# First LayerNorm's shift and scale: three of five chunks from TensorE's row matmuls to multiply-and-add on VectorE and GpSimd

## The chip, the cores and the metric

The kernel runs on one core of a Trainium2 chip. The metric is the time of one execution on the device in microseconds, as the median of several runs; smaller is better. A profiled execution gives the trace from which the rows below are taken; it has its own time, which differs a little from the median. TensorE does the matmuls (in the profile PE, and PEld for the loads of the stationary operand), VectorE is DVE, ScalarE is ACT, GpSimd is POOL; SP issues most DMAs.

## The reference

A transformer block with adaptive LayerNorm on 2048 tokens of width 640: linear attention with a Hedgehog feature map (32 heads of 20), then a dense layer with squared ReLU. What the change touches is how `h`'s shift `sa` and scale `ca` come about:

```python
x = A_x                                         # (1, 2048, 640)
mod = (_silu(c) @ w_mod).reshape(c.shape[0], 6, 1, -1)   # c: (1, 640), w_mod: (640, 3840)
sa, ca, ga, sb, cb, gb = (mod[:, 0], mod[:, 1], mod[:, 2], mod[:, 3], mod[:, 4], mod[:, 5])
h = _layernorm(x, axis=-1) * (1 + ca) + sa
x = x + ga * _A_ref(h, A_wqkv, A_w_phi, A_wo)   # q, k, v = h @ wqkv; q and k go through w_phi
h = _layernorm(x, axis=-1) * (1 + cb) + sb
x = x + gb * _B_ref(h, B_w1, B_b1, B_w2, B_b2)
```

## The kernel before

The 2048 tokens are 16 tiles of 128, worked through in pairs (8 blocks of 256); the 640 channels are 5 chunks of 128. Products are made in three passes of rounded fp32 (high by high, high by low, low by high), so each operand exists as a high part, written by ScalarE, and a low part, the difference, made by VectorE (helper `lo`, line 90).

The prologue, up to the first q matmuls, is written out by hand: under `tc.manual_schedule` each engine runs its instructions in the order of the code, and an instruction that waits holds up everything behind it on its engine. It goes so:

- `WARM` matmuls of a tile of ones (line 625) while the first weights travel.
- `fold(nm, d)`: the weights of k, then of q, chunk by chunk, are multiplied with the feature map (line 282), ScalarE takes the high part out of PSUM (line 289), VectorE the low part. The first fold waits for the block-diagonal tile `bd_t`, which VectorE builds (lines 250 and 255).
- `stats` of the first token block (lines 560 to 565: VectorE's bn_stats, then four tiny operations on GpSimd that give `sqa` and `nba`), then `scale` on ScalarE (line 570) normalises it in place.
- The shift and scale of chunk d, as two columns of `cols_a`: `w_ss` holds for each chunk a 128 x 1280 tile `WM[d]`, in which columns 256 k + 128 s + n are the weights from input chunk k to output channel n, s = 0 for the shift, 1 for the scale. `mod_rows2(d)` multiplies it with silu(c) (`cs`, one column for each k) in ten matmuls of 32 output rows each (line 586, tile `mrow`). `mod_sb(d)` copies the rows to SBUF on ScalarE (line 594, tile `msb`) and adds the 1 of (1 + ca); `mod_cols2(d)` transposes them on TensorE (line 599) and sums them on VectorE (line 601) into `cols_a`.
- `out0(d)`: ScalarE applies shift and scale to the transposed chunk (line 375, `hfa`), rounds it to the high part of `hT` (line 376), VectorE makes the low part.
- `k_step(d)`: twelve matmuls that add chunk d to the k of both token tiles (line 80, `pk`). All four PSUM buffers of the tag `pj` are in use by them; the first q matmuls (`pq`) take the first of them over, so they wait for ScalarE's eviction of k (line 433). Ahead of these evictions ScalarE has the scaling of the second token block (`scale(XB[1])`) and the high part of the first v weights (line 667).

The statistics of the second token block (`stats(XB[1], "a1")`) are written behind `k_step(1)`. The loads stand in one order on SP's queue: k weights, the first token block, q weights, `WM[0]` and `WM[1]`, the last q weights, `WM[2]` to `WM[4]`, the second token block, v weights, `b_t`. Eight semaphores are used in turn, so a load is issued only when the one eight places ahead has landed.

Of the kernel before, what the change touches and what calls it, by code (L numbers as in the profile page):

```python
# [8 lines left out]
F32 = mybir.dt.float32  # L9
# [3 lines left out]
ALU = mybir.AluOpType  # L13
AX = mybir.AxisListType

P = 128
# [6 lines left out]
NC = D // P  # L23
# [8 lines left out]
VCOLS = [*range(360), *range(600, 624), *range(360, 600), *range(624, D)]  # L32
EPS = 1e-5
POSTPONED = 4
WARM = 9
KEPT = NT - POSTPONED
W2_AT = 48
PLAIN = 2
# [15 lines left out]
def kernel(  # L54
# [19 lines left out]
    nc = tc.nc  # L74
# [14 lines left out]
    def lo(out_lo, full, hi, eng=None):  # L89
        (eng or nc.vector).tensor_tensor(out_lo, full, hi.bitcast(F32), op=ALU.subtract)  # L90
# [7 lines left out]
    const = ctx.enter_context(tc.tile_pool(name="const", bufs=1))  # L98
# [20 lines left out]
    def row(tag, name):  # L119
        return (pc if tag in ("s3", "s4") else mem).tile([P, D], F32, tag=tag, name=name, bufs=BUFS[tag])  # L120
# [4 lines left out]
    def wslot(name, tag="w", pool=None):  # L125
        return tok2(tag, name, W2_AT if name.startswith("w2_") else 0, pool).bitcast(F32R)
# [10 lines left out]
    def pj(name):  # L137
        return [psA.tile([P, 512], F32, tag="pj", name=f"{name}_{h}", bufs=4) for h in range(2)]

    def tp(name):  # L140
        return psA.tile([P, 512], F32, tag="tp", name=name)
# [10 lines left out]
    ones = const.tile([P, P], F32, name="ones")  # L152
# [19 lines left out]
    cols_a = const.tile([P, 10], F32, name="cols_a")  # L172
# [38 lines left out]
    raw, WM, RV, XB = {}, {}, {}, {}  # L211
# [10 lines left out]
    def load_x(j):  # L222
        XB[j] = tok2(f"x{j % 2}", f"xb{j}")
        nc.sync.dma_start(XB[j], x[256 * j : 256 * j + 256].rearrange("(i p) d -> p i d", p=P))
# [34 lines left out]

    cs = const.tile([P, NC], F32, name="cs")  # L260
    ce = const.tile([P, NC], F32, name="ce")
    const.tile([P, 8], F32, name="fill")
    nc.scalar.activation(ce, c_t, AF.Exp, scale=-1.0)
    nc.vector.tensor_scalar(ce, ce, 1.0, None, op0=ALU.add)
    nc.vector.reciprocal(ce, ce)
# [6 lines left out]
    def fold(nm, d, p=None):  # L272

        w = wslot(f"w{nm}{d}")
        W[nm, d] = w
        p = p or pj(f"fold{nm}{d}")
        for g, (o, n) in enumerate(GR):
            if g < 5:
                r = raw[nm][d // 2][:120, d % 2, g * P : (g + 1) * P]
            else:  # L280
                r = raw[nm][2][:120, 1, d * P : (d + 1) * P]
            nc.tensor.matmul(  # L282
                p[g // 3][:, (g % 3) * 120 : (g % 3) * 120 + n], r, bd_t[:120, g * 120 : g * 120 + n],
                start=True, stop=True,
            )

        def split():
            for h, (a, b) in enumerate(((0, 360), (360, 640))):
                nc.scalar.activation(w[:, 0, a:b], p[h][:, : b - a], AF.Copy)
                lo(w[:, 1, a:b], p[h][:, : b - a], w[:, 0, a:b])  # L290

        return split
# [68 lines left out]
    def t_in(xn, d, p, mixed=False):  # L361
        for i in range(2):
            src = by_turn(xn[:, i])[:, d] if mixed else xn[:, i, d * P : (d + 1) * P]
            nc.tensor.transpose(p[:, i * P : (i + 1) * P], src, ident)  # L364
# [7 lines left out]
    def t_out(cols, hT, d, nm, p, hf=None):  # L372
        if hf is None:
            hf = row("s3", f"hf{nm}_{d}")[:, :256]
        nc.scalar.activation(hf, p[:, :256], AF.Identity, bias=cols[:, d : d + 1], scale=cols[:, 5 + d : 6 + d])
        nc.scalar.activation(hT[:, d, 0], hf, AF.Copy)
        lo(hT[:, d, 1], hf, hT[:, d, 0])
# [43 lines left out]
    def do_v(t):  # L421
        v_out(t, proj("v", t))
# [40 lines left out]
    def do_q(t, *between):  # L463
        q_out(t, proj("q", t, *between))
# [103 lines left out]
    def scale(xt, nb, sq):  # L568
        for i in range(2):
            nc.scalar.activation(xt[:, i], xt[:, i], AF.Identity, bias=nb[:, i : i + 1], scale=sq[:, i : i + 1])  # L570

    def half(b, h):
        return kvp[b][:, 256 * h : 256 * h + 256]
# [3 lines left out]
    def mod_rows2(*ds):  # L577

        p = tp(f"mrow{ds[0]}")
        for m, d in enumerate(ds):  # L580
            MR[d] = p[:, m * P : m * P + P]
            for k in range(NC):
                for s in range(2):
                    c = 2 * (k % 2) + s
                    a = 256 * k + P * s
                    nc.tensor.matmul(  # L586
                        MR[d][32 * c : 32 * c + 32], cs[:, k : k + 1].to_broadcast([P, 32]), WM[d][:, a : a + P],
                        start=(k < 2 and m == 0), stop=(k >= NC - 2), skip_group_check=True,
                    )

    def mod_sb(*ds):
        for d in ds:
            t = MR[d, "sb"] = row("s1", f"msb{d}")[:, :P]
            nc.scalar.activation(t, MR[d], AF.Identity, bias=plus[:, 0:1])

    def mod_cols2(*ds):
        at = {d: half(0, 1)[:, P * (d % 2) : P * (d % 2) + P] for d in ds}
        for d in ds:
            nc.tensor.transpose(at[d], MR[d, "sb"], ident)
        for d, p in at.items():  # L600
            nc.vector.tensor_reduce(
                cols_a.rearrange("p (s d) -> p s d", s=2)[:, :, d],
                p.rearrange("p (h s r) -> p s h r", h=2, s=2)[:, :, :, 0], axis=AX.X, op=ALU.add,
            )

    TR = [half(0, 0), half(1, 0), half(1, 1), half(2, 0), half(2, 1)]
    mem.tile([P, 48], F32, tag="gap", name="gap", bufs=1)
    HT[0], HT[1] = ht("hT0", 0), ht("hT1", 1)
# [11 lines left out]
    def out0(d):  # L620
        t_out(cols_a, HT[0], d, "a0", TR[d])

    warm = tp("warm")
    for i in range(WARM):
        nc.tensor.matmul(warm[:, :P], ones, ones, start=True, stop=True)  # L625
# [4 lines left out]
    fold("q", 0, kvp[1:])()  # L630
    fold("q", 1)()
    scale(XB[0], *n0)
    fold("q", 2)()
    split = fold("q", 3)
    mod_rows2(0)
    mod_sb(0)
    for d in range(NC):
        t_in(XB[0], d, TR[d])
    split()
    mod_cols2(0)  # L640
    out0(0)
    mod_rows2(1)
    mod_sb(1)
    split = fold("q", 4)
    mod_cols2(1)
    split()
    mod_rows2(2)
    mod_sb(2)
    load_x(2)
    PP += [pj(f"pk{t}") for t in range(2)]  # L650
    rows_at, cols_at = {1: (3, 4)}, {1: (2,), 2: (3, 4)}
    for d in range(NC):
        mod_cols2(*cols_at.get(d, ()))
        if d + 1 < NC:
            out0(d + 1)
        if d in rows_at:
            mod_rows2(*rows_at[d])
        k_step(d)
        mod_sb(*rows_at.get(d, ()))
        if d == 1:  # L660
            n1 = stats(XB[1], "a1")
        if d == 3:
            scale(XB[1], *n1)
# [25 lines left out]
    for d in range(NC):  # L689
        t_in(XB[1], d, TR[d])  # L690
    t_out(cols_a, HT[1], 0, "a1", TR[0])
    t_out(cols_a, HT[1], 1, "a1", TR[1])
    do_q(1)
    exps(EK[1])
    k_norm(EK[0], 0)
    for d in range(2, NC):
        t_out(cols_a, HT[1], d, "a1", TR[d])
    do_v(0)
# [14 lines left out]
    for t in range(2, NT - 2):  # L713
# [13 lines left out]
        p = proj("v", t, *([(1, 0, lambda: t1(j + 1, 4))] if t == NT - 3 else []))  # L727
# [492 lines left out]
    for j in range(NB):  # L1220
# [65 lines left out]
        if j == 7:  # L1286
            t2(0, 4)
            p = tp("gbt")[:NC, :P]
# [512 lines left out]
```

## Time and profile before

| | |
|---|---|
| median of 3 runs | 751.55 us (751.29 to 751.74) |
| the profiled execution | 751.83 us, span 750.1 us |
| TensorE busy | 744.9 us, 99% of the span |
| VectorE, ScalarE, GpSimd busy | 601.4, 457.5, 169.0 us |
| granted TensorE clock | 1.0 over the span |

A row of the timeline reads: start in us from the span's start, length in us, engine, line, operation, output<-inputs, shape, how many were merged, and in brackets how long the engine was idle before and what ended that. A row of a group by line has, after the count, the busy time in us and the mean duration of one in ns, and after the second bar the idle time ahead of them with its cause. In rows of a single line three durations stand as least/median/most. A fp32 matmul shows as two passes, so x20 is ten matmuls.

### The profile page before, as it was taken

The numbers are of one execution on the slowest core, as the hardware profiler recorded it, in microseconds if no ns is written. First come the engines' busy times: TensorE is split into PE (matmuls) and PEld (weight loads), VectorE is DVE, ScalarE is ACT, GpSimd is POOL, SyncE is SP. The second block draws the span as 40 slices with busy tenths as digits, with TensorE's granted clock in tenths as the row PEclk, the third lists the DMA queues.
The fourth block names the chain that finished last, engine by engine and source line by source line (L and its number), as shares of the span: only waits on it lengthen the run. The fifth ranks groups of instructions, "written<-read, shape, count | busy, mean of one in ns | idle before, by whom it ended". The sixth has DMA issues, their size and how long they took to land.

```text
span 750.1 us, 15320 instructions
## 1 busy us (share of the span) xinstructions
PE 744.9 (99%) x5854; PEld 728.3 (97%) x5854; DVE 601.4 (80%) x1089; ACT 457.5 (61%) x1065; POOL 169.0 (23%) x355
## 2 busy tenths in 40 slices
PE   9999999999999999999999999999999999999998
PEld 9999999999999998998999999999999999999997
DVE  6598987988998899999665778777777776777766
ACT  5767666667863355557587766475574756647431
POOL 3000101000100237647303040132221313223110
PEclk9999999999999999999999999999999999999999
DMA  9811432343432254663885576797667767667461
GB/s 330 335 36 77 155 93 81 107 140 107 137 101 81 57 189 160 150 148 109 195 236 183 158 212 227 252 343 204 180 198 200 222 183 227 191 172 218 127 184 36
DMA packets 58796, 126.39 MB, mean 168 GB/s; under 512 B 7438, under 2 KB 16403, under 8 KB 58723
## 3 DMA queue, kind: packets, MB, share of 16 engines
q1 hardware_dynamic: 38636, 79.20, 32.2%
q0 software_dynamic: 17504, 40.90, 21.8%
q10 hardware_dynamic: 2583, 5.30, 1.9%
q8 instruction: 46, 0.75, 0.4%
q14 instruction: 27, 0.22, 0.1%
HBM read 100.74 MB, written 29.89 MB: 174 GB/s over the span
## 4 chain that ended last, share of the span: by engine, by line
PE 98%; ACT 1%; DVE 1%; POOL 0%; issue 0%; ACTq 0%; POOLq 0%
PE up L80 25%; PE acc L80 18%; PE pq L80 9%; PE pk L80 9%; PE pv L80 9%; PE pwo L80 9%; PE acc3x L80 5%; PE kvp L457 3%; PE te L954 2%; PE numa L80 1%; PE foldk L282 1%; PE numb L80 1%; PE ta L364 1%; PE foldq L282 1%; PE warm L625 1%; PE mrow L586 1%
## 5 line engine op out<-in xcount | busy, mean ns | idle before, releaser
L80 PE MATMUL up<-h,w 128*128 128x256 f32 x1640 | 204.6, 276 | 0.1
L80 PEld LDWEIGHTS up<-h,w 128*128 128x128 f32 x1640 | 196.5, 188 | 0.7 <-DVE h L90 0.5
L1350 ACT ACTIVATE ft<-up,b_t 128x256 f32<-128x256 f32 x104 | 49.0, 471 | 96.0 <-PE up L80 95.6
L80 PE MATMUL acc<-w,ra 128*128 128x384 f32 x452 | 97.5, 335 | 0.0
L80 PE MATMUL pwo<-wo,ot 128*128 128x384 f32 (+1 forms) x480 | 78.4, 314 | 0.0
L1351 DVE TENSOR_TENSOR ft<-ft 128x256 f32<-128x256 f32 x104 | 43.8, 421 | 43.1 <-ACT ft L1350 41.4
L80 PE MATMUL pq<-wq,hT 128*128 128x384 f32 (+1 forms) x480 | 75.6, 312 | 0.0
L80 PEld LDWEIGHTS acc<-w,ra 128*128 128x128 f32 x452 | 72.7, 188 | 0.8 <-DVE ra L90 0.6
L80 PE MATMUL pk<-wk,hT 128*128 128x384 f32 (+1 forms) x480 | 72.7, 308 | 0.0
L80 PEld LDWEIGHTS pwo<-wo,ot 128*128 128x128 f32 x480 | 69.7, 188 | 2.8 <-issue 2.7
L80 PEld LDWEIGHTS pq<-wq,hT 128*128 128x128 f32 x480 | 71.1, 188 | 0.6 <-issue 0.2
L80 PE MATMUL pv<-wv,hT 128*128 128x384 f32 (+1 forms) x480 | 71.6, 306 | 0.0
L80 PEld LDWEIGHTS pk<-wk,hT 128*128 128x128 f32 x480 | 70.5, 188 | 0.4 <-issue 0.2
L80 PEld LDWEIGHTS pv<-wv,hT 128*128 128x128 f32 x480 | 70.0, 188 | 0.0
L90 DVE TENSOR_TENSOR ra<-ft,ra 128x384 fp32r<-128x384 f32 (+2 forms) x86 | 36.8, 449 | 32.6 <-ACT ra L1374 20.0
L1460 POOL DMA_DIRECT2D ring_a<-td_a x34 | 18.5, 543 | 116.9 <-PE acc L80 103.6
L1374 ACT ACTIVATE ra<-ft 128x384 fp32r<-128x384 f32 x48 | 25.2, 526 | 28.4 <-DVE ft L1351 22.4
L80 PE MATMUL acc3x<-w,ra 128*128 128x256 f32 x231 | 39.5, 278 | 0.0
L80 PEld LDWEIGHTS acc3x<-w,ra 128*128 128x128 f32 x231 | 37.2, 188 | 0.0
L1365 DVE TENSOR_TENSOR ft<-ft 128x128 f32<-128x128 f32 x136 | 33.3, 286 | 1.2
L448 DVE TENSOR_REDUCE sk<-ek 128x64 f32<-128x1280 f32 x16 | 23.7, 1484 | 12.8 <-ACT ek L443 10.8
L341 POOL TENSOR_SCALAR sma<-sma 128x2 f32<-128x2 f32 x6 | 1.8, 298 | 137.2 <-ACT xb L340 137.2
(270 smaller groups left out, 1470.2 us busy)
## 6 DMA issues: line engine op xcount, KB each, us to landing
ring_c<-td_c POOLq DMA_DIRECT2D x34, 384.0 KB, 3.8
ring_a<-td_a POOLq DMA_DIRECT2D x34, 384.0 KB, 3.4
ring_b<-td_b POOLq DMA_DIRECT2D x34, 256.0 KB, 3.6
esp<-eq SPq DMA_DIRECT2D x12, 640.0 KB
el<-esp SPq DMA_DIRECT2D x12, 640.0 KB
rw<-in_w SPq DMA_DIRECT2D x23, 320.0 KB
wm<-in_w_mod SPq DMA_DIRECT2D x20, 320.0 KB
xb<-in_x SPq DMA_DIRECT2D x8, 640.0 KB
```

The costliest lines, as they stand in the source:

```text
L80: nc.tensor.matmul(o, a, b, start=first and i == 0, stop=last and i == len(terms) - 1, skip_group_check=skip,)
L90: (eng or nc.vector).tensor_tensor(out_lo, full, hi.bitcast(F32), op=ALU.subtract)
L282: nc.tensor.matmul(p[g // 3][:, (g % 3) * 120 : (g % 3) * 120 + n], r, bd_t[:120, g * 120 : g * 120 + n], start=True, stop=True,)
L364: nc.tensor.transpose(p[:, i * P : (i + 1) * P], src, ident)
L448: nc.vector.tensor_reduce(s, heads(flat(e)), axis=AX.X, op=ALU.add)
L457: nc.tensor.matmul(kvp[g // 4][64 * c : 64 * c + 64, a : a + 2 * n].rearrange("p (s n) -> p s n", s=2), v[:, u], e[:, :, o : o + n], start ...
L954: nc.tensor.transpose(p[:124, a : a + P], EU[2 * j + i][:, 2 * g + c, :124], ident)
L1350: nc.scalar.activation(r, p, AF.Relu, bias=b1_t[:, f : f + 1])
L1351: nc.vector.tensor_tensor(r, r, r, op=ALU.mult)
L1365: nc.vector.tensor_tensor(t[:, o], t[:, a], t[:, b], op=op)
L1374: nc.scalar.activation(a[:, 0, :3], t[:, :3], AF.Copy)
L1460: nc.gpsimd.dma_start(RING[j, n, r], TD[n][r].bitcast(F32R))
```

## The change

Chunks 0 and 1 keep the old way. For chunks 2, 3 and 4 the five products over k are made elementwise: `mod_acc` multiplies the 256 columns of each k by the column of `cs` that belongs to it and sums them into the first 256 columns of `WM[d]`, in place. VectorE does so for chunks 2 and 4 (one multiplication, four fused multiply-adds each), GpSimd for chunk 3 (five multiplications, four additions). `mod_col` then sums over the partitions: two matmuls with 128 columns of `WM[d]` as stationary operand and one column of ones moving, and VectorE adds 0 to the shift and 1 to the scale (`unit`, two tiny fills on GpSimd) on the way to `cols_a`. The row blocks, copies and transposes of these chunks go. `WARM` falls from 9 to 8.

```diff
-WARM = 9
+WARM = 8
...
-    const.tile([P, 8], F32, name="fill")
+    unit = const.tile([P, 8], F32, name="unit")
+    nc.gpsimd.memset(unit[:, :1], 0.0)
+    nc.gpsimd.memset(unit[:, 1:2], 1.0)
...
+    def mod_acc(d, eng, *ks):
+        acc = WM[d][:, :256]
+        for k in ks:
+            if k == 0:
+                eng.tensor_scalar(acc, acc, cs[:, 0:1], None, op0=ALU.mult)
+            elif eng is nc.gpsimd:
+                t = WM[d][:, 256 * k : 256 * k + 256]
+                eng.tensor_scalar(t, t, cs[:, k : k + 1], None, op0=ALU.mult)
+                eng.tensor_tensor(acc, acc, t, op=ALU.add)
+            else:
+                t = WM[d][:, 256 * k : 256 * k + 256]
+                eng.scalar_tensor_tensor(acc, t, cs[:, k : k + 1], acc, op0=ALU.mult, op1=ALU.add)
+
+    def mod_col(d):
+        p = half(0, 1)[:, P + 8 * d : P + 8 * d + 2]
+        for s in range(2):
+            nc.tensor.matmul(
+                p[:, s : s + 1], WM[d][:, P * s : P * s + P], ones[:, :1], start=True, stop=True, skip_group_check=True
+            )
+        nc.vector.tensor_tensor(
+            cols_a.rearrange("p (s d) -> p s d", s=2)[:, :, d], p, unit[:, :2], op=ALU.add
+        )
...
     scale(XB[0], *n0)
+    mod_acc(3, nc.gpsimd, *range(NC))
     fold("q", 2)()
+    mod_acc(2, nc.vector, 0)
     split = fold("q", 3)
...
     mod_cols2(0)
+    mod_acc(2, nc.vector, 1, 2)
     out0(0)
+    mod_acc(2, nc.vector, 3)
     mod_rows2(1)
     mod_sb(1)
     split = fold("q", 4)
     mod_cols2(1)
     split()
-    mod_rows2(2)
-    mod_sb(2)
     load_x(2)
     PP += [pj(f"pk{t}") for t in range(2)]
-    rows_at, cols_at = {1: (3, 4)}, {1: (2,), 2: (3, 4)}
     for d in range(NC):
-        mod_cols2(*cols_at.get(d, ()))
+        if d == 0:
+            mod_acc(2, nc.vector, 4)
         if d + 1 < NC:
             out0(d + 1)
-        if d in rows_at:
-            mod_rows2(*rows_at[d])
+        if d == 0:
+            mod_acc(4, nc.vector, 0, 1, 2, 3)
+        if d == 1:
+            mod_acc(4, nc.vector, 4)
         k_step(d)
-        mod_sb(*rows_at.get(d, ()))
+        if d + 2 < NC:
+            mod_col(d + 2)
         if d == 1:
             n1 = stats(XB[1], "a1")
```

What stands where on VectorE before, from the low parts of fold q3 (`wq_356`) to the statistics of the second token block:

```order
L90 TENSOR_TENSOR wq_356<-foldq_0_357,wq_356 128x360
L90 TENSOR_TENSOR wq_356<-foldq_1_358,wq_356 128x280
L601 TENSOR_REDUCE cols_a<-kvp_76 128x2
L90 TENSOR_TENSOR hT_225<-hfa_0_394,hT_225 128x256
L601 TENSOR_REDUCE cols_a<-kvp_76 128x2
L90 TENSOR_TENSOR wq_411<-foldq_0_412,wq_411 128x360
L90 TENSOR_TENSOR wq_411<-foldq_1_413,wq_411 128x280
L90 TENSOR_TENSOR hT_225<-hfa_1_445,hT_225 128x256
L601 TENSOR_REDUCE cols_a<-kvp_76 128x2
L90 TENSOR_TENSOR hT_225<-hfa_2_463,hT_225 128x256
L560 BN_STATS sta_504<-xb_165 128x6 x2
```

The three reductions are those of chunks 0, 1 and 2; between the last of them and the statistics stands one low part of `hT`.

The first part of the same stretch on VectorE after, up to the third shift-and-scale (`wm_159` is chunk 2, `wm_163` chunk 4; fold q3 is now `wq_367`):

```order
L612 TENSOR_SCALAR wm_159<-wm_159,cs 128x256
L90 TENSOR_TENSOR wq_367<-foldq_0_368,wq_367 128x360
L90 TENSOR_TENSOR wq_367<-foldq_1_369,wq_367 128x280
L603 TENSOR_REDUCE cols_a<-kvp_76 128x2
L619 SCALAR_TENSOR_TENSOR wm_159<-wm_159,cs 128x256 x2
L90 TENSOR_TENSOR hT_227<-hfa_0_407,hT_227 128x256
L619 SCALAR_TENSOR_TENSOR wm_159<-wm_159,cs 128x256
L603 TENSOR_REDUCE cols_a<-kvp_76 128x2
L90 TENSOR_TENSOR wq_425<-foldq_0_426,wq_425 128x360
L90 TENSOR_TENSOR wq_425<-foldq_1_427,wq_425 128x280
L619 SCALAR_TENSOR_TENSOR wm_159<-wm_159,cs 128x256
```

The first multiplication of chunk 2 now stands ahead of the low parts of fold q3, and the four sums of chunk 2 stand between the work of chunks 0 and 1.

What follows on VectorE after, up to the same statistics:

```order
L90 TENSOR_TENSOR hT_227<-hfa_1_447,hT_227 128x256
L612 TENSOR_SCALAR wm_163<-wm_163,cs 128x256
L619 SCALAR_TENSOR_TENSOR wm_163<-wm_163,cs 128x256 x3
L627 TENSOR_TENSOR cols_a<-kvp_76,unit 128x2
L90 TENSOR_TENSOR hT_227<-hfa_2_470,hT_227 128x256
L619 SCALAR_TENSOR_TENSOR wm_163<-wm_163,cs 128x256
L627 TENSOR_TENSOR cols_a<-kvp_76,unit 128x2
L562 BN_STATS sta_490<-xb_165 128x6 x2
```

Chunk 4's multiplication and three sums stand ahead of chunk 2's addition, and its last sum and chunk 3's addition ahead of the statistics, which were behind the low part of `hT` alone.

On GpSimd after, `wm_161` being chunk 3, between the two sets of statistics:

```order
L567 TENSOR_SCALAR nba_294<-nba_294 128x2
L612 TENSOR_SCALAR wm_161<-wm_161,cs 128x256
L615 TENSOR_SCALAR wm_161<-wm_161,cs 128x256
L616 TENSOR_TENSOR wm_161<-wm_161 128x256
L615 TENSOR_SCALAR wm_161<-wm_161,cs 128x256
L616 TENSOR_TENSOR wm_161<-wm_161 128x256
```

Two more such pairs follow, and then the four operations of the second token block's statistics; before, GpSimd had nothing between the two.

## The prediction

> **What bounds the kernel now.** I read the page first, for the engine that carries the span, then the chain that ended last, then the rows in order of time around the change, and at last the waits of the DMA queue.
>
> The page, its busy times and the shares of the chain:
>
> ```profile
> PE 744.9 (99%) x5854; PEld 728.3 (97%) x5854; DVE 601.4 (80%) x1089; ACT 457.5 (61%) x1065; POOL 169.0 (23%) x355
> PE 98%; ACT 1%; DVE 1%; POOL 0%; issue 0%; ACTq 0%; POOLq 0%
> ```
>
> TensorE never rests, so any microsecond by which its queue is held up in the prologue is a microsecond at the end, and any that it is relieved of can be won only if nothing else is late. The chain in order of time (start, length, what), at the blocks that the change removes and at the first matmuls behind them:
>
> ```profile
> 22.44 0.78 PE mrow L586 x20
> ...
> 25.26 1.44 PE mrow L586 x40
> ...
> 28.62 0.22 PE kvp L599 x2
> 28.83 5.18 PE pk L80 x36
> ```
>
> That chain names TensorE alone. A second one runs beside it with no slack; it is seen in the rows in order of time (start, length, engine, line):
>
> ```profile
> 19.52 0.89 DVE L90 TENSOR_TENSOR wq<-foldq,wq 128x360 fp32r<-128x360 f32 x2 [0.56 <-ACT wq L289]
> ...
> 20.33 0.15 DVE L601 TENSOR_REDUCE cols_a<-kvp 128x2 f32<-128x4 f32 x1
> 20.52 0.56 ACT L375 ACTIVATE hfa<-kvp,cols_a 128x256 f32<-128x256 f32 x1 [0.74 <-DVE cols_a L601]
> ...
> 21.43 0.35 ACT L594 ACTIVATE msb<-mrow,plus 128x128 f32<-128x128 f32 x1
> ...
> 22.02 0.22 PEld L599 LDWEIGHTS kvp<-ident,msb 128*128 128x128 f32 x1
> ...
> 25.30 0.16 DVE L601 TENSOR_REDUCE cols_a<-kvp 128x2 f32<-128x4 f32 x1 [0.30 <-PE kvp L599]
> ...
> 26.54 0.42 DVE L90 TENSOR_TENSOR hT<-hfa,hT 128x256 fp32r<-128x256 f32 x1 [1.08 <-ACT hT L376]
> ...
> 26.88 0.88 DVE L560 BATCH_NORM_STATS2 sta<-xb 128x6 f32<-128x320 f32 x2
> ...
> 30.68 0.23 POOL L565 TENSOR_SCALAR nba<-nba 128x2 f32<-128x2 f32 x1
> ...
> 30.94 1.74 ACT L570 ACTIVATE xb<-xb,nba,sqa 128x640 f32<-128x640 f32 x2
> ...
> 32.59 0.72 ACT L667 ACTIVATE wv<-rawv 128x640 fp32r<-128x640 f32 x1
> 33.21 1.39 ACT L433 ACTIVATE k<-pk 128x384 f32<-128x384 f32 x4
> 33.74 4.37 PEld L80 LDWEIGHTS pq<-wq,hT 128*128 128x128 f32 x30
> ```
>
> Read it backwards. The first q matmul (33.74) writes the PSUM buffer that the first k eviction on ScalarE empties; the four evictions start at 33.21, and the first is done at 33.21 + 1.39/4 or a little more, some 33.6 to 33.7. They stand behind wv (32.59), that behind the scaling of the second token block (30.94), that waits for GpSimd's nba (30.68 + 0.23 = 30.91), and that for the statistics which VectorE began at 26.88. From 26.88 to 33.74 are **6.86 us without slack**. Whatever makes VectorE begin those statistics later makes q, and the kernel, later.
>
> The DMA queue tells when the modulation weights are there. In the program each load on it waits for the one eight places ahead; the fifth rawv and b_t stand eight behind the wm of chunks 2 and 3. Its rows in order of time, and its waits:
>
> ```profile
> 20.43 0.33 SPq L246 DMA_DIRECT2D rawv<-in_wv  x1
> 22.02 0.33 SPq L514 DMA_DIRECT2D b_t<-in_b  x1
> ...
> SPq L514 <- DMA wm<-in_w_ss: 1.2, 1, 1.2
> SPq L246 <- DMA wm<-in_w_ss: 1.2, 1, 1.2
> ```
>
> So chunk 2 landed at 20.4 and chunk 3 at 22.0. TensorE used them at 22.4 and 25.3, late enough not to notice.
>
> **The change part by part.** Prices of the operations, by groups, by single lines, and in order of time:
>
> ```profile
> L1351 DVE TENSOR_TENSOR ft<-ft 128x256 f32<-128x256 f32 x104 | 43.8, 421 | 43.1 <-ACT ft L1350 41.4
> L298 DVE SCALAR_TENSOR_TENSOR wm<-wm,cs,wm 128x640 f32<-128x640 f32 x16 | 14.1, 878 | 0.2
> L440 DVE TENSOR_TENSOR ek<-k,mxk 128x640 f32<-128x640 f32 x32 | 25.1, 818 | 0.8 <-PE kvp L457 0.7
> L296 DVE TENSOR_SCALAR wm<-wm,cs 128x640 f32<-128x640 f32 x4 | 2.2, 548 | 0.0
> L1356 DVE SCALAR_TENSOR_TENSOR ft<-ft x8: 416/416/420, 428.1 to 741.4; 64x256 f32<-64x256 f32 x8
> L891 POOL TENSOR_TENSOR dn<-dn,rs_q x16: 317/322/1496, 258.3 to 356.1; 128x64 f32<-128x64 f32 x16
> L893 POOL TENSOR_TENSOR dd<-dd,dn x32: 249/253/1449, 259.9 to 356.8; 128x32 f32<-128x32 f32 x32
> 1.77 0.29 POOL masks.py:199 TENSOR_SCALAR_AFFINE_SELECT ident<-ident 128x128 f32<-128x128 f32 x1
> 266.01 0.52 PEld L942 LDWEIGHTS tail<-kvd,ept 80*128 80x128 f32 x4
> 1.05 4.21 PE L625 MATMUL warm<-ones 128*128 128x128 f32 x18 [1.05 <-POOL bdc L157]
> 4.84 7.61 PEld L282 LDWEIGHTS foldk<-bd_t,raw_k 120*128 120x128 f32 x60
> 13.74 4.19 PE L282 MATMUL foldq<-bd_t,raw_q 120*128 120x120 f32 x36
> 4.17 0.89 DVE L250 TENSOR_TENSOR bd_t<-bdc 120x360 f32<-120x360 f32 x2 [1.91 <-POOL mask L195]
> ```
>
> *TensorE.* Removed: the row blocks of chunks 2, 3, 4 (0.78 + 1.44) and three transposes (some 0.11 each, 0.22 for two): 2.55 us. Added: three pairs of one-column matmuls with a full 128x128 stationary operand. Each pair is four weight loads; the row of four such loads with short moving operands gives 0.52, less the overlap at the end 0.45. No row has a moving operand of one column; the low end is the pace of the row blocks, 0.78/20 a pass, 0.16 a pair. I take 0.45, since the weights are full. Sum 1.35, so TensorE is relieved of **1.2 us** (up to 2.1).
>
> *The warm-up matmul.* Two passes of the 18 that end where the first fold matmul starts, near 5.05 (18 of them in 4.21, with the overlap of the last): (5.05 - 1.05)/18 x 2 = 0.44 at most; but the first fold needs bd_t, whose first part (the longer of two in 0.89) ends near 4.7, and its weights were loading at 4.84 already: 0.1 is left. Step 1 below starts from a landing, which does not move with TensorE, so I enter **0** (bounds 0 and -0.4).
>
> *VectorE, step 1.* The first multiplication of chunk 2 stands ahead of the low parts of fold q3 and waits for chunk 2's landing, 20.43. Its price lies between 0.22 (0.548 scaled to 256 columns) and 0.42 (two inputs); I take 0.35, nearer the upper since a fixed part does not scale. The low parts then run at 20.7 instead of 19.52, and the reduction behind them at 21.53 instead of 20.33: 1.2 later. ScalarE's hfa follows at 21.7, and msb of chunk 1, queued behind it, 0.9 later at 22.6 (the distance 20.52 to 21.43); its 0.35 and the hop give the transposes at 23.0 instead of 22.02, so TensorE stands still for 1 us, and the second reduction comes at 23.5. The one row block saved there gives most of it back: k step 0 starts at 23.4 against 23.2.
>
> *Step 2.* Ahead of chunk 2's final addition VectorE has, from 23.5: the reduction, the low parts of fold q4 (0.9), the last sum of chunk 2, the low part of hT 1 (next after 0.34), then chunk 4's multiplication and three sums. A sum over 256 columns costs between 0.416 (L1356) and 0.48 (0.421, and the 0.06 by which a sum is longer than a two-input operation at 640 columns, 878 against 818); I take 0.48, since L298 takes its factor from a tensor as here, and 0.51 to the next, which needs its result. That is 24.4, 24.8, 25.1, 25.5, 26.0, 26.5, and the addition at 26.9; it was 25.30. TensorE's pair for it is done by 25.6, so VectorE alone sets this.
>
> *Step 3.* From there by hfa, hT and its low part to the statistics were 26.88 - 25.30 = 1.6; that ends at 28.5, and now chunk 4's last sum and chunk 3's addition stand in between: 0.48. The statistics begin at 28.9 to 29.0, **2.0 later**, and q likewise. With the lower prices (five sums at 0.06 less, two multiplications at 0.13 less) it is 1.4, with the upper (two at 0.07 more) 2.2. TensorE's k steps end by 34.5 in this count, before the eviction lets q start, so their relief is swallowed.
>
> *GpSimd.* Chunk 3: five multiplications and four additions from 22.0. The two-input price grows by 0.069 for 32 columns (253 to 322), so 0.74 at 256; the one-input price I put at 0.4, above the 0.29 of 128 columns. With hops 5.2 us: done at 27.2 if left alone, just when TensorE gets there (23.4 + 2 x 1.75 + 0.45). The two zero and one fills cost 0.1 each, behind work that nobody waits for. But it isn't left alone. GpSimd's nba (its duration as least, median, most, then first and last start) took 0.195 at 15.4 and 0.417 at 30.2, where a VectorE operation on two SBUF tensors was under way (30.11 to 30.54); and a 128x64 sum took 1.50 instead of 0.32:
>
> ```profile
> L564 POOL TENSOR_TENSOR nba<-mva,sqa x2: 195/306/417, 15.4 to 30.2; 128x2 f32<-128x2 f32 x2
> 30.11 0.43 DVE L90 TENSOR_TENSOR hT<-hfa,hT 128x256 fp32r<-128x256 f32 x1 [1.01 <-ACT hT L376]
> 258.12 1.48 DVE L884 TENSOR_TENSOR scr<-el,zb 128x1280 f32<-128x1280 f32 x1
> 258.28 1.50 POOL L891 TENSOR_TENSOR dn<-dn,rs_q 128x64 f32<-128x64 f32 x1 [8.39 <-DVE dn L886]
> ```
>
> The latter ended 0.18 after VectorE's operation (258.28 + 1.50 against 258.12 + 1.48), more than half of its own 0.32: GpSimd does its reading only when VectorE is through. From 22.0 to chunk 3's addition VectorE has 4.7 us of such operations (three sums of chunk 2, three low parts of hT at 0.34, one multiplication and four sums of chunk 4) and GpSimd about 4.1 (four at 0.6, five at 0.34, without the dispatch). One after the other they end at 30.8 instead of 28.9; the low parts of fold q4 and ScalarE's hops overlap with some of it. I take **1.5**, ends 0 (they don't meet) and 2.9 (GpSimd gets only what VectorE leaves: 28.95 - 22.0 - 4.7 = 2.25 by then, the other 1.85 behind it, and TensorE's pair and hops after that).
>
> The Trainium skill (SBUF — State Buffer, Who interferes with whom) states an exclusive lock: whichever of the two started first holds the shared port for its whole instruction and the other fully blocks. By that rule VectorE's sums wait in turn and the sum is 2.0 + 1.5; with GpSimd alone waiting, which is all that these rows show, it would be 2.0 + 2.6 to 2.9.
>
> The sum: 2.0 + 1.5 + 0 = 3.5 us on the profiled 751.83, whose span is 750.1; that run is 0.28 above the median of 751.55, so on the median it is **755.0**.
>
> **The rivals.** *No contention:* GpSimd finishes at 27.2 beside VectorE. For it: the rows that collide have other shapes, and a sum of few columns can slip in between two of VectorE's. Against it: 1.50 for 0.32. Then the 1.4 to 2.2 stand alone, 753.0 to 753.8.
>
> *Short waits:* chunk 2 lands earlier beside what the queue's row tells (the load's last piece decides, and no row shows the others), and the sums are at their low price. Step 1 falls away (its 1.2, of which 0.9 reaches the statistics): 0 to 1.3 later, 751.6 to 752.9.
>
> *Faster, the other side:* the second chain doesn't bind, and TensorE keeps its relief of 1.2 to 2.1: 749.5 to 750.4. It decides when the statistics start no later than 26.88 less the gain, 24.8 to 25.7; for that VectorE would need to skip 3 us of work queued ahead of them. That the chain names TensorE throughout speaks for it; that q at 33.74 follows the eviction within 0.1 speaks against.
>
> *Much slower:* the warm-up, now ended before bd_t is there, leaves a gap, TensorE's full pace comes later than before (a pass took 4.21/18 = 0.23 in the warm-up and 4.19/36 = 0.12 in the q folds), or the stalls of 1 to 3 us lower it again. Each microsecond at half pace costs 0.5: 3 us more would be 1.5, over 756.6.
>
> **How the numbers follow.** Contention 0.45 (754.2 to 756.6), no contention 0.27, short waits 0.13, faster 0.07, much slower 0.08. The range from 751.6 to 756.6 holds the first three, 0.85; the likeliest alone has 754.2 to 756.6. About 0.2%, 1.5 us, is what a measurement of this kernel can tell from no change. Faster by more: the 0.07. Within: short waits and a trace of the next, 0.15. Slower: 0.78.
>
> **What would show it.** Step 1 is right if VectorE is idle until 20.4 ahead of the first multiplication, released by the load, and the transposes of chunk 1 start near 23.0. Steps 2 and 3: statistics at 29 or later. GpSimd: its additions at well over 0.74, and TensorE idle behind k step 1 until they end. The chain should name VectorE, GpSimd and ScalarE between 21 and 37, and q should start at 37 instead of 33.74. Wrong I am if the q matmuls start by 34, or if the evictions do not release them.

## The result, and the profile after

The changed kernel takes 757.33 us (median of six runs, 756.62 to 758.32) against 751.54 of the kernel before beside it: 1.0079 times as long, interval 1.0068 to 1.0090. It is slower, as forecast, but by 5.8 us instead of 3.5, and outside the range. The profiled execution took 758.32 us with a span of 756.6, 1 us above the median; in its code the lines stand two lower than before (560 is now 562).

The page, its busy times and the shares of the chain:

```profile
PE 745.9 (99%) x5801; PEld 728.6 (96%) x5801; DVE 606.6 (80%) x1099; ACT 456.6 (60%) x1062; POOL 177.7 (23%) x366
PE 93%; DMA 3%; POOL 1%; ACT 1%; DVE 1%; issue 0%; ACTq 0%; DVEq 0%
```

TensorE has as much busy time as before, but its share of the chain fell from 98 to 93%. The chain in order of time (start, length, what) shows what took its place:

```profile
12.58 10.48 DMA wm<-in_w_ss
...
23.15 1.21 POOL wm L612
...
25.50 0.97 POOL wm L616
26.47 1.08 POOL wm L615
...
31.23 0.73 POOL wm L616
...
32.00 0.62 PE kvp L624 x4
...
32.65 0.16 DVE cols_a L627
32.81 0.80 DVE sta L562 x2
...
36.83 1.74 ACT xb L572 x2
...
39.61 1.48 PE pq L80 x7
```

From chunk 3's landing to 31.96 the kernel hangs on GpSimd; then TensorE's pair, VectorE's addition, the statistics, the scaling, the eviction, and q. VectorE's rows in order of time (start, length, engine, line, operation, in brackets the idle time ahead), and TensorE's transposes of chunk 1 and its pair of chunk 3:

```profile
21.50 0.35 DVE L612 TENSOR_SCALAR wm<-wm,cs 128x256 f32<-128x256 f32 x1 [3.33 <-DMA wm<-in_w_ss]
...
22.57 0.15 DVE L603 TENSOR_REDUCE cols_a<-kvp 128x2 f32<-128x4 f32 x1
...
25.80 0.96 DVE L90 TENSOR_TENSOR hT<-hfa,hT 128x256 fp32r<-128x256 f32 x1
...
29.18 0.15 DVE L627 TENSOR_TENSOR cols_a<-kvp,unit 128x2 f32<-128x2 f32 x1
...
32.65 0.16 DVE L627 TENSOR_TENSOR cols_a<-kvp,unit 128x2 f32<-128x2 f32 x1 [1.28 <-PE kvp L624]
32.72 0.88 DVE L562 BATCH_NORM_STATS2 sta<-xb 128x6 f32<-128x320 f32 x2
```

```profile
24.08 0.33 PE L601 MATMUL kvp<-ident,msb 128*128 128x128 f32 x1 [2.20 <-ACT msb L596]
...
32.00 0.61 PE L624 MATMUL kvp<-ones,wm 128*128 128x1 f32 x4 [2.10 <-POOL wm L616]
```

VectorE idles 3.33 us ahead of chunk 2's first multiplication, until the load is there at 21.5 (20.43 in the profile before); the addition of chunk 2 follows at 29.18, chunk 3's addition waits for TensorE's pair and that for GpSimd; the statistics start at 32.72 instead of 26.88, q at 39.61 instead of 33.74: 5.87 later. From statistics to q it is 6.89 us, 6.86 before.

GpSimd's groups and VectorE's sums (count, busy, mean ns), and the busy time by window (after the window's length PE, PEld, DVE, ACT, POOL, then the granted clock, the DMA share and GB/s):

```profile
L615 POOL TENSOR_SCALAR wm<-wm,cs 128x256 f32<-128x256 f32 x4 | 4.2, 1047 | 0.0
L616 POOL TENSOR_TENSOR wm<-wm 128x256 f32<-128x256 f32 x4 | 3.2, 788 | 0.3
```

```profile
L619 DVE SCALAR_TENSOR_TENSOR wm<-wm,cs 128x256 f32<-128x256 f32 x8 | 4.3, 537 | 0.1
```

```profile
20.00:25.00 5.00, 2.80 (x30) 2.49 (x23) 3.30 (x10) 2.16 (x6) 1.85 (x2) 0.98 1.01 399
25.00:30.00 5.00, 4.91 (x25) 4.71 (x24) 4.22 (x9) 1.31 (x4) 4.75 (x6) 0.68 1.05 386
```

GpSimd's nine operations took 8.8 us; the forecast had 5.2 for them alone. Behind TensorE's wait of 2.2 us its clock fell as well.

### The profile page after: what moved, and what is told of

Same layout as the page of the kernel before. It is cut to its first block, busy times and chain, and to the rows that moved or that the text cites. A ratio compares the mean times of both kernels' runs of the same rounds, so it can differ in the third digit from the quotient of the medians.

```text
span 756.6 us, 15229 instructions
## 1 busy us (share of the span) xinstructions
PE 745.9 (99%) x5801; PEld 728.6 (96%) x5801; DVE 606.6 (80%) x1099; ACT 456.6 (60%) x1062; POOL 177.7 (23%) x366
## 4 chain that ended last, share of the span: by engine, by line
PE 93%; DMA 3%; POOL 1%; ACT 1%; DVE 1%; issue 0%; ACTq 0%; DVEq 0%
PE up L80 24%; PE acc L80 18%; PE pq L80 9%; PE pv L80 9%; PE pwo L80 9%; PE pk L80 8%; PE acc3x L80 5%; PE kvp L459 3%; PE te L984 2%; DMA wm<-in_w_ss 1%; PE numa L80 1%; DMA raw_q<-in_wq 1%; PE numb L80 1%; PE ta L366 1%; POOL wm L615 1%; DMA bdc<-in_bd 0%
## 5 line engine op out<-in xcount | busy, mean ns | idle before, releaser
L80 PE MATMUL pk<-wk,hT 128*128 128x384 f32 (+1 forms) x480 | 74.5, 312 | 0.0
```

The source lines that it names most:

```text
L80: nc.tensor.matmul(o, a, b, start=first and i == 0, stop=last and i == len(terms) - 1, skip_group_check=skip,)
```

## The experiments

Each was timed beside the kernel before; times are medians, ratios are to the kernel before, with intervals. Since the landing of chunk 2 differs from run to run, the traces are compared by the distance from VectorE's first multiplication of chunk 2, which follows the landing, to the statistics.

| kernel | time, us | ratio | multiplication | statistics | distance | q |
|---|---|---|---|---|---|---|
| the changed kernel | 757.33 | 1.0079 (1.0068 to 1.0090) | 21.50 | 32.72 | 11.22 | 39.61 |
| no_gpsimd | 754.64 | 1.0046 (1.0031 to 1.0061) | 20.95 | 29.45 | 8.50 | 36.34 |
| mul_behind_fold | 753.27 | 1.0022 (1.0014 to 1.0031) | 20.33 | 27.83 | 7.50 | 34.72 |
| all_vector | 756.29 | 1.0074 (1.0057 to 1.0090) | 21.29 | 31.63 | 10.34 | 38.52 |
| after_tt | 757.95 | 1.0079 (1.0065 to 1.0093) | 21.48 | 32.80 | 11.32 | 39.68 |
| after_tt_mul | 756.20 | 1.0057 (1.0044 to 1.0069) | 21.55 | 31.47 | 9.92 | 39.15 |
| stats_ahead | 757.97 | 1.0084 (1.0071 to 1.0097) | 20.27 | 30.08 | 9.81 | 39.79 |
| stats_fill | 757.75 | 1.0085 (1.0071 to 1.0099) | 20.99 | 30.80 | 9.81 | 38.25 |
| after_fill | 759.42 | 1.0095 (1.0081 to 1.0109) | 20.50 | 31.73 | 11.23 | 38.62 |

**One warm-up matmul less, alone** (warm8_only):

```diff
-WARM = 9
+WARM = 8
```

> The kernel before with nothing changed but one warm-up matmul less (8 instead of 9). My price for it was 0 (0 to -0.4 us), so 751.1 to 751.6, with k's first fold near 4.75 instead of 4.84 and TensorE's clock at 1.0 throughout. The rival: the shorter warm-up leaves a gap ahead of the folds or lets the granted clock fall later; then TensorE shows a window under 0.9 in the first 30 us and the time is 752 to 753. It would also show whether the loads land a microsecond later (chunk 2 at 21.4 instead of 20.4) because of the earlier folds: by that theory they do so here, by the theory that this is chance or comes from other parts they land near 20.4.

751.82 us beside 751.61, ratio 0.9998 (0.9989 to 1.0007): worth nothing, as priced. Its rows of the DMA queue, each issued when chunk 2 and chunk 3 had landed:

```profile
21.47 0.33 SPq L246 DMA_DIRECT2D rawv<-in_wv  x1
23.07 0.33 SPq L514 DMA_DIRECT2D b_t<-in_b  x1
```

Here too the loads came 1.05 us later than in the profile before (20.43 and 22.02), with none of the new operations there, and it cost nothing. But mul_behind_fold, which has the eight matmuls as well, found chunk 2 at 20.33: the landing scatters between 20.3 and 21.6 from run to run. The kernel before has slack for that; the changed one has not, and my count took one early landing for the rule.

**GpSimd's work left out**, and with it chunk 3's sum over k (no_gpsimd):

```diff
-    mod_acc(3, nc.gpsimd, *range(NC))
```

> The changed kernel without GpSimd's nine operations: chunk 3's sum over k is left out (its columns come from the weights of k = 0, unweighted). Theory: GpSimd's chain delays the statistics twice, by blocking VectorE (the low part of hT 0.96 instead of 0.42, three sums 1.99 instead of 1.45, a multiplication 0.56 instead of 0.35: 1.3 us) and by its own late end, for which chunk 3's addition on VectorE waits 1.3 us ahead of the statistics. Without it the addition of chunk 2 comes near 27.9 instead of 29.2, the statistics near 30.1 instead of 32.7, and the kernel takes 757.3 - 2.6 = 754.7; 1 us less, 753.7, if the loads land as early as in the kernel before. The rival, that VectorE's own queue (the wait for chunk 2's landing and ten sums) sets it all: 756.8 to 757.4. With GpSimd alone blocked and VectorE not, the price of the end wait only: 756.0.

754.64, as expected. VectorE's first and last row, and the group of its sums:

```profile
20.95 0.35 DVE L612 TENSOR_SCALAR wm<-wm,cs 128x256 f32<-128x256 f32 x1 [1.86 <-DMA wm<-in_w_ss]
29.45 0.88 DVE L562 BATCH_NORM_STATS2 sta<-xb 128x6 f32<-128x320 f32 x2
```

```profile
L619 DVE SCALAR_TENSOR_TENSOR wm<-wm,cs 128x256 f32<-128x256 f32 x8 | 3.8, 480 | 0.1
```

The distance is 8.50 us; the forecast's steps 1 to 3 gave 28.95 less 20.43, 8.5. So VectorE's part was counted right, and GpSimd's costs 2.7 us, by the times (757.33 less 754.64) and by the distances (11.22 less 8.50).

**The first multiplication behind the low parts of fold q3**, GpSimd's work left out as before (mul_behind_fold):

```diff
-    mod_acc(2, nc.vector, 0)
     split = fold("q", 3)
...
-    mod_acc(2, nc.vector, 1, 2)
+    mod_acc(2, nc.vector, 0, 1, 2)
```

> The changed kernel without GpSimd's nine operations (chunk 3's sum over k is left out, as in no_gpsimd), and with chunk 2's first multiplication moved behind the low parts of fold q3 and the first reduction, so that nothing on VectorE waits for chunk 2's landing ahead of them. Theory (step 1 of the forecast): the wait costs the reduction 1.2 us plus whatever the load lands after 20.4, of which 0.9 or more reaches the statistics; so the reduction comes at 20.3, the transposes of chunk 1 at 22.0, the statistics near 28.5 instead of 29.45, and the kernel takes 753.3 to 753.9 against 754.6 of no_gpsimd. The rival: VectorE's sums are the bound anyway and only close up, so the time stays 754.3 to 754.9.

```profile
20.33 0.35 DVE L612 TENSOR_SCALAR wm<-wm,cs 128x256 f32<-128x256 f32 x1 [0.34 <-DMA wm<-in_w_ss]
...
27.83 0.88 DVE L562 BATCH_NORM_STATS2 sta<-xb 128x6 f32<-128x320 f32 x2
```

753.27, 1.4 less than no_gpsimd, of which 1.0 is in the distance and the rest in an earlier landing. Taken off in this order, the 5.8 us split into 2.7 for GpSimd, 1.4 for the low parts and transposes held up behind a load, and 1.7 (753.27 less 751.54) that remain. I put these down to the sums that still stand ahead of the statistics; the trace shows 0.95 of them there (27.83 instead of 26.88), and no run shows where the rest is.

**Chunk 3 alone, on GpSimd** (only_gpsimd), in the kernel before:

```diff
-    rows_at, cols_at = {1: (3, 4)}, {1: (2,), 2: (3, 4)}
+    rows_at, cols_at = {1: (4,)}, {1: (2,), 2: (4,)}
...
+    mod_acc(3, nc.gpsimd, *range(NC))
...
+        if d == 1:
+            mod_col(3)
```

> The kernel before with chunk 3 alone made the new way, on GpSimd; chunks 2 and 4 by row matmuls, nine warm-up matmuls. VectorE has no sums here, so little blocks GpSimd. Theory: GpSimd's multiplication by a column of factors itself costs 0.9 to 1.0 us for 256 columns, not the 0.4 of the forecast, and an addition 0.72: 22.0 + 5 x 0.95 + 4 x 0.75 = 29.8, the addition on VectorE at 30.4, the statistics behind it at 30.5 instead of 26.9, so the kernel takes 755.0 to 755.4. The rival (they cost 0.4 alone and were only held up by VectorE's work): done at 27.2 to 27.6, statistics near 28.2, 752.8 to 753.2.

```profile
L615 POOL TENSOR_SCALAR wm<-wm,cs 128x256 f32<-128x256 f32 x4 | 3.7, 930 | 0.0
L616 POOL TENSOR_TENSOR wm<-wm 128x256 f32<-128x256 f32 x4 | 2.9, 727 | 0.3
```

With VectorE nearly idle a multiplication by a column takes 0.93 us, an addition 0.73 (0.74 forecast), the nine 7.8 us: of the 8.8 in the changed kernel only 1.0 is VectorE's doing. The time, 756.89 (1.0074, 1.0062 to 1.0086), is above the 755.0 to 755.4 that I gave: chunk 3 landed at 22.9 instead of 22.0, and behind a wait of 3.3 us TensorE's last three k steps took 7.01 us, which the next run did in 5.61.

**The same with another form of multiplication** (gpsimd_tt; the one for k = 0 is changed alike):

```diff
-                eng.tensor_scalar(t, t, cs[:, k : k + 1], None, op0=ALU.mult)
+                eng.tensor_tensor(t, t, cs[:, k : k + 1].to_broadcast([P, 256]), op=ALU.mult)
```

> As only_gpsimd (chunk 3 alone on GpSimd, 756.9 us), but the five multiplications take the factor as a second operand, the column of cs repeated over the 256 columns, instead of as a scalar for each partition. There a multiplication by the scalar took 0.93 with VectorE idle and an addition 0.72. Theory: the form makes the price, so a multiplication now takes 0.72 like the addition; five of them save 1.0, the statistics start at 30.6 instead of 31.6, 755.6 to 756.2. The rival: GpSimd pays for reading a column by column factor whatever the form, 0.9 or more: 756.6 to 757.2, or slower.

```profile
22.46 0.61 POOL L615 TENSOR_TENSOR wm<-wm,cs 128x256 f32<-128x256 f32 x1
...
24.61 0.94 DVE L90 TENSOR_TENSOR hT<-hfa,hT 128x256 fp32r<-128x256 f32 x1 [1.14 <-ACT hT L378]
```

755.03 (1.0050, 1.0036 to 1.0064) is lower than the 755.6 to 756.2 expected. A multiplication takes 0.61 (at 22.46 and 23.84; up to 0.81 beside VectorE's work), so the form with a factor for each partition made the price. The difference of the two times is not that price alone: in the profiled runs GpSimd started at 21.85 here and at 22.96 in only_gpsimd, 1.1 us of landing. And VectorE's low part of hT 1 beside GpSimd took 0.94 instead of 0.42.

**That form in the changed kernel** (after_tt; the edit is the same):

> The changed kernel with GpSimd's five multiplications written with the factor as a second operand (the column of cs repeated over the 256 columns), nothing else. In the changed kernel each took 0.92 to 1.21 us; in gpsimd_tt this form took 0.61 to 0.81. Theory: the price of those five is the term of the forecast that was far too small, and GpSimd's end sets the statistics; then 5 x 0.35 = 1.7 us less on GpSimd, the statistics near 31 instead of 32.7 for the same landing, 755.3 to 756.0 instead of 757.3. The rival: VectorE, which waits for GpSimd's port time in any form, is the bound: 756.7 to 757.5.

GpSimd's groups and VectorE's sums, and VectorE's addition of chunk 2:

```profile
L618 POOL TENSOR_TENSOR wm<-wm 128x256 f32<-128x256 f32 x4 | 3.1, 776 | 0.3
L617 POOL TENSOR_TENSOR wm<-wm,cs 128x256 f32<-128x256 f32 x4 | 3.0, 758 | 0.0
```

```profile
L621 DVE SCALAR_TENSOR_TENSOR wm<-wm,cs 128x256 f32<-128x256 f32 x8 | 5.6, 700 | 0.1
```

```profile
30.76 0.15 DVE L629 TENSOR_TENSOR cols_a<-kvp,unit 128x2 f32<-128x2 f32 x1
```

My theory fell: 757.95, no gain. GpSimd was done at 30.04 instead of 31.95, but VectorE's eight sums took 0.70 each (0.48 alone, 0.54 in the changed kernel), and its addition of chunk 2 came at 30.76 instead of 29.18. What one engine gained the other lost.

**Both repairs together** (after_tt_mul: after_tt, with the edit of mul_behind_fold):

> As after_tt, and chunk 2's first multiplication moved behind the low parts of fold q3, as in mul_behind_fold, where it was worth 1.4 us with GpSimd idle. Theory: GpSimd starts when chunk 3 lands, wherever VectorE stands, and ends some 6.7 us later, 28.7 to 29.8, so the addition of chunk 3 and the statistics come near 29.5 to 30.5 whatever VectorE has gained: 754.2 to 755.2, only 0.5 to 1.2 less than after_tt. The rival: the two repairs add up, 1.4 less than after_tt or more: 753.9 or less.

756.20, 1.75 less than after_tt: more than the first theory gave, which had GpSimd as the bound, and near the rival's sum; its bound of 753.9 counted from a base that after_tt had not reached. VectorE sets the statistics here, as there; but q follows them by 7.7 us instead of 6.9, since TensorE, which had waited in pieces, made k steps 1 and 2 in 3.55 us each, so a part of the gain went to its clock (in the profiled run, which at 757.36 was the slowest of five).

**Chunk 3 on VectorE as well** (all_vector):

```diff
-    mod_acc(3, nc.gpsimd, *range(NC))
...
+        if d == 1:
+            mod_acc(3, nc.vector, 0, 1)
         if d + 1 < NC:
             out0(d + 1)
...
         if d == 1:
+            mod_acc(3, nc.vector, 2, 3, 4)
             mod_acc(4, nc.vector, 4)
```

> The changed kernel with chunk 3's product on VectorE too (one multiplication, four sums at 0.35 and 0.48 us, two of them in the gap ahead of the low part of hT 2, three ahead of chunk 4's last sum), nothing on GpSimd. Theory: GpSimd and VectorE, both on SBUF, mostly take turns, so that GpSimd's nine operations of 7.8 us cost the statistics 2.7 us, more than the same product would cost VectorE itself: statistics 8.5 + 3 x 0.48 = 9.9 us behind chunk 2's landing instead of 11.2, the kernel 754.6 + 1.4 = 756.0 (755.6 to 756.4) against 757.3. The rival: GpSimd does work beside VectorE, which the split makes use of, and all on VectorE is as slow or slower: 757.0 or more.

```profile
21.29 0.35 DVE L612 TENSOR_SCALAR wm<-wm,cs 128x256 f32<-128x256 f32 x1 [2.61 <-DMA wm<-in_w_ss]
...
31.63 0.88 DVE L562 BATCH_NORM_STATS2 sta<-xb 128x6 f32<-128x320 f32 x2
```

756.29: with all three chunks on one engine the statistics come 0.9 us sooner behind the load than with the work split over two. By the times the gain is near 1 us, but the intervals of the two ratios overlap, so the distance carries this more than the clock does. That the split brings no gain is shown; that the two engines only take turns is not, since GpSimd's 7.8 us cost 2.7.

**The statistics ahead of chunk 3** (stats_ahead):

```diff
+        if d == 1:
+            n1 = stats(XB[1], "a1")
         if d + 2 < NC:
             mod_col(d + 2)
-        if d == 1:
-            n1 = stats(XB[1], "a1")
```

> The changed kernel with the statistics of the second token block written ahead of chunk 3's column matmuls and addition, not behind. Theory: the statistics set when q starts (6.9 us later), so they now begin where VectorE comes free of chunk 4's last sum, 31.4 instead of 32.7; the addition of chunk 3 moves back some 0.8 and k steps 3 and 4 with it, which still end in time. q near 38.4 instead of 39.6, the kernel 756.1 to 756.4. The rival: TensorE's k steps, late through GpSimd, set q as well, so that it gains nothing or loses: 757.0 to 758.0.

The statistics, TensorE's k step 2, and its window:

```profile
30.08 0.87 DVE L562 BATCH_NORM_STATS2 sta<-xb 128x6 f32<-128x320 f32 x2
...
31.67 3.55 PE L80 MATMUL pk<-wk,hT 128*128 128x384 f32 x12
```

```profile
30.00:35.00 5.00, 4.21 (x16) 4.21 (x17) 2.56 (x9) 0.98 (x2) 2.29 (x5) 0.50 0.96 361
```

The rival held: 757.97. The statistics came 1.4 sooner behind the load, and q no sooner: TensorE, idle for 3.5 us, went on at half pace, and its k steps became the bound, with ScalarE's hT 4 and the scaling queued behind them.

**Fillers in that wait** (stats_fill: 14 matmuls of ones ahead of chunk 3's pair) and in the changed kernel's (after_fill: nine):

```diff
+        if d == 1:
+            busy = tp("busy")
+            for i in range(14):
+                nc.tensor.matmul(busy[:, :P], ones, ones, start=True, stop=True)
         if d + 2 < NC:
             mod_col(d + 2)
```

> As stats_ahead (758.0 us), with 14 matmuls of the tile of ones in TensorE's queue where it waits for GpSimd's chunk 3, written to a buffer that nobody reads. In stats_ahead TensorE stood still from 27.3 to 30.8, the granted clock was 0.50 from 30 to 35, and k step 2 took 3.55 us instead of 2.0; the statistics, at 30.1, were early enough and TensorE was not. Theory: the idle stretch made the clock fall. Then the fillers (some 3 us) keep it at 1.0, step 2 takes 2.0, its end and all that follows come 1.5 to 2.0 earlier, 755.9 to 756.6. The rival: the clock falls for another reason (heat, the load of the engines), the fillers change nothing: 757.5 to 758.5.

> The changed kernel with nine matmuls of the tile of ones in TensorE's queue behind k step 1, where it waits for GpSimd's chunk 3 (2.1 us there). Question: does the fall of the granted clock cost the changed kernel time? Theory: no, the statistics on VectorE set q by way of ScalarE and TensorE waits in any case: 757.0 to 757.8. The rival: where the load lands earlier the wait is over 3 us, the clock falls to half behind it, as in stats_ahead, and TensorE becomes the bound by 0.5 to 1.3: then the fillers bring 756.0 to 756.8.

K step 2 of stats_fill, and a wait in the second half of the kernel, in the squared ReLU (us, times, longest):

```profile
31.99 1.99 PE L80 MATMUL pk<-wk,hT 128*128 128x384 f32 x12
```

```profile
PE acc L80 <- ACT ft L1384: 0.6, 1, 0.6
```

The fillers did what they should in both profiles (clock 1.0 in every window, k step 2 at 1.99 instead of 3.55, q at 38.25 instead of 39.79), and the times did not follow. stats_fill took 757.75 against 757.97: a time that the rival gave, though the clock did not fall, as the rival had it. after_fill took 759.42 against 757.33, where neither theory had it. In stats_fill 0.6 us of the gain is lost again in the wait shown; in three of after_fill's four runs 2.7 us lie outside the span instead of 1.7. Why is open, and so is what the clock's fall costs the changed kernel; in its profiled run it cost nothing, since q follows the chain of VectorE and ScalarE there.

**Chunk 3 alone, on VectorE, in its idle time** (one_on_vector, in the kernel before), **and then without the waits that this placing made** (k4_before_k3). The second's order, shortened, with `part` giving the statistics of one token tile at a time:

```diff
+    mod_acc(3, nc.vector, 0, 1)
+    out0(1); mod_acc(3, nc.vector, 2, 3); k_step(0)
+    mod_cols2(2); mod_acc(3, nc.vector, 4); next(part)
+    out0(2); mod_rows2(4); k_step(1); mod_sb(4)
+    n1 = list(part)[-1]
+    mod_cols2(4); out0(4); k_step(2)
+    mod_col(3); out0(3); k_step(4)
+    scale(XB[1], *n1); k_step(3)
```

> The kernel before with chunk 3 alone made the new way, on VectorE, its five sums put where VectorE had idle time (behind the low parts of fold q4 and of hT 1), and the statistics of the second token block cut in two, the first token tile ahead of the low part of hT 2, the second behind chunk 3's addition. Nothing stands ahead of the statistics that wasn't there, and TensorE is relieved of a row block and a transpose for a pair of one-column matmuls (0.3 to 0.4 us). Theory: what the change cost came from the work ahead of the statistics and not from the new way itself, so this takes 751.2 to 751.7, no difference to the kernel before. The rival: the sums hurt wherever they are (by VectorE's low parts or TensorE's pair): 752.5 or more.

> As one_on_vector (752.7 us), with what held its statistics up taken away: their second half follows the low part of hT 2 at once, not behind chunk 3's addition and chunk 4's reduction (they waited 0.66 and 0.48 us for TensorE there), and k step 4 is made before k step 3, so that chunk 3's columns are needed 1.7 us later. Theory: with nothing ahead of the statistics that wasn't there before, the time is that of the kernel before, 751.2 to 751.9. The rival: the new way costs something in itself: 752.5 or more.

The second token tile's statistics, of one_on_vector with the wait ahead of them, of k4_before_k3, and the latter's scaling:

```profile
28.64 0.17 DVE L627 TENSOR_REDUCE cols_a<-kvp 128x2 f32<-128x4 f32 x1 [0.48 <-PE kvp L625]
28.72 0.88 DVE L562 BATCH_NORM_STATS2 sta<-xb 128x6 f32<-128x320 f32 x2
```

```profile
27.81 0.88 DVE L562 BATCH_NORM_STATS2 sta<-xb 128x6 f32<-128x320 f32 x2
...
31.57 1.72 ACT L573 ACTIVATE xb<-xb,nba,sqa 128x640 f32<-128x640 f32 x2
```

one_on_vector: 752.72 (1.0016, 1.0008 to 1.0025), a miss: I had put the second half behind an addition and a reduction that wait for TensorE, 0.66 and 0.48 us. k4_before_k3 has it at 27.81, 752.60 beside 751.98 (1.0010, 1.0001 to 1.0019): a difference that can hardly be told from none, but above the 751.2 to 751.9 that I expected, and where the rival, that the new way costs something in itself, had it. One delay is seen: now the scaling stands on ScalarE behind hT 3, at 31.57 instead of 30.94. Whether that is all of it is open. So a chunk in the new way can be had for 0.1 to 1.4 us, but no version ran faster than the kernel before.

## Why the forecast was wrong in size

*The chain.* Right: statistics to q stayed at 6.9 us in the changed kernel, and a delay ahead of them came out at the end: from q to the end of the span it is 716.1 to 717.7 us in all fifteen traces. TensorE's relief was swallowed. The pair of one-column matmuls took 0.50 at full clock (0.45 forecast).

*The warm-up.* Right: 0. The first fold started at 4.74, released by bd_t.

*VectorE, steps 1 to 3.* Right from the landing on, with sums at 0.48 and multiplications at 0.35: without GpSimd chunk 2's addition came 6.46 us behind the landing (27.41 less 20.95; 26.9 less 20.43 is 6.47) and the statistics 8.50 (8.5). In the changed kernel the transposes came at 24.08 instead of 23.0 for the landing alone, the addition at 29.18 instead of 26.9 for that and 1.2 us of waiting for GpSimd. Step 1 was to cost the statistics 0.9, and mul_behind_fold shows 1.0 in the distance. Wrong in its start: 20.43 is one landing out of a scatter up to 21.6, some 0.5 early against the mean of the nine in the table, 21.0, and the sum had nothing for that.

*GpSimd: the step that failed.* The term was 1.5 (0 to 2.9) and measured 2.7: within its bounds, but 1.2 above the value that entered the sum. GpSimd's own time was priced at 5.2 us, with the multiplication at 0.4 from a row of another operation over 128 columns; by a column of factors it takes 0.93, the nine 7.8. So GpSimd is late without any contention too, at 30.8 when it starts at 23.0, and the rival by which it finishes in time at no cost could not have come true.

The 1.5 stood for two engines that take turns, with chunk 3's addition behind both. Of the 2.7, 1.2 came from VectorE's waiting in turn: the low part of hT 1 took 0.96 instead of 0.42, and with chunk 4's multiplication and three sums it brought chunk 2's addition 7.68 us behind the landing, against 6.46 without GpSimd. The other 1.5 lies between that addition and the statistics, 3.54 us instead of 2.04: there chunk 3's addition waited 1.28 us for the pair that GpSimd's late end had held up. The right price alone would not have mended the forecast: in after_tt GpSimd's end no longer sets the statistics, which are again 2.04 us behind chunk 2's addition; but that addition comes 9.28 us behind the landing instead of 6.46, and the cost is 2.8. The Trainium skill (SBUF — State Buffer, Who interferes with whom), which I cited with 2.0 + 1.5, has either engine wait for the other's whole instruction. That VectorE waits too is what after_tt shows, where sums went from 0.48 to 0.70 while GpSimd's operations took 0.78; whether for a whole instruction, these means do not tell.

In the profiled pair the landing was 1.07 us later, and 1.07 + 2.0 + 2.7 are 5.8 of the 5.87 by which q is late. For the medians, with 0.5 for the landing, the sum is 5.2 of the 5.8 measured. The other 0.6 is not attributed.

*The rivals.* The time fell into "much slower", but not by its mechanism: the clock did fall, and did not set q in the profiled run.

## What to carry to other kernels

Before work is moved to an idle engine, price it on that engine in the very form (operation, operands, shape); a row of another operation over half the columns was off by a factor of 2.3. Look also at what it does to the engine beside it: in after_tt the cheaper form gained nothing, since VectorE lost as much. Then ask what stands behind it in order on a queue that the end depends on: here a delay of the statistics came out at the end, and an operation that waits for a load, put ahead of ready work, cost 1.4 us. A load time from one profile is one draw: if a step is to start from it, look at several.

## What the runs showed of the hardware

GpSimd's multiplication of 128x256 by one factor for each partition took 0.93 us, by the same factor as a repeated second operand 0.61, an addition 0.73. The slow form is the better neighbour: beside it VectorE's sums averaged 0.54, beside the fast one 0.70. VectorE's low parts of the q folds, which read one operand from PSUM, took 0.52 to 0.53 over 360 columns in the changed kernel, in after_tt and in no_gpsimd alike; those of fold q4 ran beside GpSimd in the first two.

TensorE's granted clock fell behind waits of 2.2 us (the changed kernel, 0.68 over five microseconds, that is 3.2 of them at half, and 0.2 more in the stretch ahead, at 0.98) and 3.5 us (stats_ahead, 0.50), but not behind one of 2.5 (all_vector, 1.0). In after_tt_mul, where TensorE's last waits ahead of it were 0.97 and 0.62 us, it was 0.56 and 0.50 in the two stretches of 5 us from 25 to 35. So the length of one wait does not decide it here. The Trainium skill (TensorE: Matmul & The Clock Gate, What's actually happening) tells of half pace after at least one idle window of about 3.4 us, and of a window that runs free, so that the moment of a change depends on where in it the work lands. The 3.4 us at half pace in the changed kernel agree with the window; that a wait of 2.2 us was enough does not agree with a whole idle window. Whether the clock falls differs from run to run: no_gpsimd's four runs with a mean clock of 1.0 have spans of 752.1 to 753.2 us, the two with 0.995 and 0.998 of 755.6 and 755.1.
